# A scheduled attention and feed-forward kernel: eight DMA lanes in the plan, another load order, a PSUM bank for the rest's x, and q's exponential row by row

## The chip, the cores and the metric

The kernel runs on one core of one Trainium2 chip. The metric is the device time of one execution in microseconds (us). Five engines work side by side, each through its own instruction stream in order: TensorE (PE in the profile; its weight loads are PEld), VectorE (DVE), ScalarE (ACT), GpSimd (POOL) and SyncE (SP), which issues most of the DMA transfers.

## The reference

Four batches of eight heads, 576 tokens, 64 dimensions per head, everything in 32-bit floats:

```
q_s = softmax(q, over the 64 dims);  k_s = softmax(k, over the 576 tokens)
kv  = k_s^T v            (64 x 64 for each head);   x = q_s kv
x   = (silu(x w_gate) * (x w_val)) w_out            2304 x 512 -> 1536 -> 512
out = ((x w_a) * (x w_b)) w_out2                    2304 x 512 -> 1536 -> 512
```

The q that is put in has a spread of 0.8, k and v have one of 0.1.

## The kernel before

**Tiling.** The tokens are cut into five blocks: 512 of each batch, and the four "rests" of 64 tokens together. The first layer (l = 0) takes its blocks in the order batch 0, 1, 2, the rests, batch 3; the second (l = 1) in the order 0, 1, 2, 3, rests. In a block the hidden dimension of 1536 goes by in 12 tiles f. For each f TensorE makes two products `u_l_i_f_0` and `u_l_i_f_1` (12 matmuls of 512 columns each, since every operand is split into a high and a low part and three products are added), ScalarE and VectorE make the gated h from them (silu `s`, product into the second `u`, high part by an ACT cast, low part by a DVE subtraction), and four groups of three matmuls add h to the accumulators `acc` (the down product). The two u of a tile have one PSUM bank each, gv0 and gv1. The down product of f stands behind the two u of f + 1.

**Weights.** Each tile of weights arrives as 64-bit floats (`wr`, two halves of 768 columns, two 32-bit words each) and is converted once per layer: ACT takes an absolute value (`a<-wr`, L363) and scales the low words (`wr<-wr`, L367), DVE clamps, shifts and joins (L369, L372, L375), POOL or DVE adds (L380), then the high part is an ACT cast and the low part a subtraction on DVE or POOL (`w<-a`, L298 and L292). In the first block this conversion runs beside the products that need its result.

**Attention.** `attend(b, g, ...)` does two heads: four groups g for each batch b. Its tiles are `ut` for b < 2 and `ua`, `uc`, `uq` later. On PE: `kx` and `kb` (the maximum of k turned round), `kv`, `qt` and `ql` (q turned round), `xt` (x of 512 tokens), `xl` (x of the rest). Batch 0 runs before the first block; batch 1 is mixed into the first block, batch 2 into the second, batch 3 into the third. ACT, which computes both exp and silu, loads a function table when it changes from one to the other.

**Order.** Nothing runs in the order in which the code adds it. `Plan.add` collects operations with an estimated cost, `Plan.prepare` gives each a due time, counted back from its users and from a wanted time (`due=`), and `Plan.order` plays the engines forward in estimated time, always taking the operation that can start first, and among those the one due first. That gives each engine's order and the PSUM bank of each buffer that has several tags. On the chip each engine then runs its stream in order and waits for semaphores. Loads on SP keep the order in which the code adds them (`after=last_load`). The framework has eight DMA semaphores, and a transfer's issue waits until the one eight before has landed.

Of the kernel before, what the change touches and what calls it, by code (L numbers as in the profile page):

```python
# [30 lines left out]
class Plan:  # L31
# [11 lines left out]
    SLACK = 0.7  # L43
    DMA_START, DMA_END, DMA_RATE = 1.1, 0.95, 300e3
    TABLE = 1.3
# [69 lines left out]
    def order(self):  # L115
# [34 lines left out]
        while len(done) < len(ops):  # L150
# [27 lines left out]
            if op["table"] and op["table"] != table:  # L178
                table, t = op["table"], t + self.TABLE
            free[engine] = t + cost  # L180
            if op["nbytes"]:
                dma_free = max(dma_free, t + self.DMA_START) + op["nbytes"] / self.DMA_RATE
                end[n] = dma_free + self.DMA_END
            elif engine == "tensor":
                window = int(t / self.WINDOW)
                used[window] = used.get(window, 0.0) + cost
                full = used.get(window - 1, 0.0) > 0.3735 * self.WINDOW
                free[engine] = end[n] = t + cost * (1 if full else 2)
            else:
                end[n] = t + cost  # L190
# [21 lines left out]
def kernel(  # L212
# [201 lines left out]
    def attend(b, g, xhl, due):  # L414
# [57 lines left out]
        def qraw():  # L472
            return col(Q, q0, n)
# [90 lines left out]
        for o, x, y, keys, key, width in less:  # L564
# [11 lines left out]
        add("gpsimd", pool_us(m, BROADCAST), lambda: nc.gpsimd.tensor_tensor(
            out=qx(), in0=qraw()[:, 0:m].rearrange("p (h r d) -> p r h d", h=HG, r=R),
            in1=st()[:, 0, 0:G].rearrange("p (h r) -> p r h", h=HG).unsqueeze(3).to_broadcast([P, R, HG, D]),
            op=ALU.subtract), [QR, (st, "max")], [Q_])
        add("gpsimd", pool_us(P, BROADCAST), lambda: nc.gpsimd.tensor_tensor(  # L580
            out=ql(), in0=qr_(), in1=st()[:, 0, G:G + 1].to_broadcast([P, P]), op=ALU.subtract),
            [*QRL, (st, "maxl")], [(A, "ql")])
# [19 lines left out]
        for h in range(HG):  # L602
# [16 lines left out]
        add("vector", 0.17, lambda: nc.vector.tensor_scalar(
            out=st()[:, 2, :], in0=st()[:, 1, :], scalar1=EPS, scalar2=None, op0=ALU.add), [st], [st])  # L620
        add("vector", 0.21, lambda: nc.vector.reciprocal(out=st()[:, 3, :], in_=st()[:, 2, :]), [st], [st])  # L621
        add("gpsimd", pool_us(n, BROADCAST), lambda: nc.gpsimd.tensor_tensor(  # L622
            out=qg(), in0=qg(), in1=st()[:, 3, :].unsqueeze(2).to_broadcast([P, GX, D]), op=ALU.mult),
            [Q_, QL, st], [Q_, QL])
        pt, pl = psum([P, R, P], "qt", f"acc{g}"), psum([P, SL], "ql")
# [236 lines left out]
```

## Time and profile before

| | |
|---|---|
| median of 3 runs | 1008.91 us (1008.12 to 1010.12) |
| the profiled execution's own time | 1010.94 us |
| its span, first to last instruction | 1009.1 us |
| PE busy | 966.9 us (96%) |
| DVE, ACT, POOL busy | 411.6, 347.8, 188.1 us |
| granted TensorE clock, mean | 0.987 |

PE is busy for nearly all of the span, so its idle time is what there is to look for. It lies almost wholly ahead of 171 us, where the other three engines are busiest. Times of rows count from the span's start; between the profiled execution's time and its span lie 1.8 us.

### The profile page before, as it was taken

How to read it: one execution, taken by the hardware profiler on the slowest of the kernel's cores; microseconds unless marked ns; L12 is line 12 of the kernel's file. 1: busy time of each engine (PE TensorE's matmuls, PEld its weight loads, DVE VectorE, ACT ScalarE, POOL GpSimd, SP SyncE). 2: the span in 40 equal slices, each digit the busy share in tenths (PEclk: the TensorE clock that was granted, in tenths of full speed). 3: DMA queues.
4: the chain of work that ended last, by engine and by line, in shares of the span. 5: the costliest groups of instructions: out<-in, count | busy, mean ns of one | idle time of the engine just before them, and what ended most of it. 6: DMA issues, size and time to landing. Idle time of an engine off the chain costs nothing.

```text
span 1009.1 us, 12039 instructions
## 1 busy us (share of the span) xinstructions
PE 966.9 (96%) x4616; PEld 799.8 (79%) x4616; DVE 411.6 (41%) x702; ACT 347.8 (34%) x556; POOL 188.1 (19%) x206
## 2 busy tenths in 40 slices
PE   5679989999999999999999999999999999999997
PEld 4467667888878888898888888888888888888897
DVE  6678797433233333424666763221121112211212
ACT  5665666333332334313455551211121112111211
POOL 5654453111111110200444341000000000000000
PEclk9879999999999999999999999999999999999999
DMA  9732544210131112501334630020001001000100
GB/s 275 242 105 72 178 141 148 90 45 28 33 120 48 47 47 94 180 1 63 121 126 129 186 118 0 1 84 1 1 21 64 1 0 42 21 1 1 42 1 22
DMA packets 77137, 74.18 MB, mean 74 GB/s; under 512 B 29976, under 2 KB 64280, under 8 KB 76184
## 3 DMA queue, kind: packets, MB, share of 16 engines
q1 hardware_dynamic: 71416, 69.36, 22.3%
q10 hardware_dynamic: 5664, 4.07, 1.2%
q8 instruction: 36, 0.59, 0.2%
q14 instruction: 21, 0.17, 0.1%
HBM read 60.29 MB, written 13.11 MB: 73 GB/s over the span
## 4 chain that ended last, share of the span: by engine, by line
PE 82%; DMA 1%; ACT 1%; DVE 1%; issue 1%; POOL 0%; SPq 0%; ACTq 0%; POOLq 0%; DVEq 0%
PE u L707 53%; PE acc L737 15%; PE acc L734 12%; DMA wr<-in_moe_w_out_dram 1%; PE kv L594 1%; PE xt L642 1%; DMA out_dram<-ob 0%; PE qt L629 0%; DVE xhl L292 0%; PE kv L595 0%; PE ql L632 0%; DVE ob L750 0%; ACT wr L367 0%; ACT xhl L298 0%; SPq L341 0%
## 5 line engine op out<-in xcount | busy, mean ns | idle before, releaser
L707 PE MATMUL u<-xhl,w 128*128 128x512 f32 (+1 forms) x2856 | 625.1, 373 | 7.4 <-DVE w L292 4.4
L707 PEld LDWEIGHTS u<-xhl,w 128*128 128x128 f32 x2856 | 498.5, 190 | 105.0 <-DVE w L292 4.2
L721 DVE TENSOR_TENSOR u<-s,u 128x512 f32<-128x512 f32 (+1 forms) x120 | 77.1, 643 | 425.7 <-PE u L707 388.9
L718 ACT ACTIVATE s<-u 128x512 f32<-128x512 f32 (+1 forms) x120 | 66.8, 557 | 301.0 <-PE u L707 299.6
L734 PE MATMUL acc<-h,w 128*128 128x512 f32 (+1 forms) x720 | 167.3, 379 | 0.4 <-DVE h L292 0.2
L737 PE MATMUL acc<-w,h 128*128 128x512 f32 x648 | 157.4, 392 | 0.0
L734 PEld LDWEIGHTS acc<-h,w 128*128 128x128 f32 x720 | 125.0, 189 | 27.8 <-issue 1.9
L737 PEld LDWEIGHTS acc<-w,h 128*128 128x128 f32 x648 | 120.9, 188 | 25.6
L298 ACT CAST h<-u 128x512 fp32r<-128x512 f32 (+1 forms) x120 | 65.3, 544 | 208.3 <-DVE u L721 206.9
L380 POOL TENSOR_TENSOR a<-a,wr 128x768 uint32<-128x768 uint32 (+1 forms) x48 | 95.6, 1993 | 184.8 <-DVE a L375 165.7
L292 DVE TENSOR_TENSOR h<-u,h 128x512 fp32r<-128x512 f32 (+1 forms) x120 | 76.3, 635 | 50.1 <-ACT h L298 49.8
L292 POOL TENSOR_TENSOR xhl<-xraw,xhl 128x512 fp32r<-128x512 f32 (+1 forms) x6 | 7.3, 1220 | 340.7 <-ACT xhl L298 243.9
L375 DVE SCALAR_TENSOR_TENSOR a<-wr,a 128x768 uint32<-128x768 uint32 (+1 forms) x49 | 58.1, 1188 | 0.7
L367 ACT ACTIVATE wr<-wr 128x768 uint32<-128x768 uint32 (+1 forms) x49 | 43.8, 895 | 12.2 <-DMA wr<-in_moe_w_out_dram 12.1
L363 ACT ACTIVATE a<-wr 128x768 f32<-128x768 f32 (+1 forms) x40 | 35.5, 888 | 25.4 <-DMA wr<-in_moe_w_out_dram 22.4
L298 ACT CAST w<-a 128x768 fp32r<-128x768 f32 (+1 forms) x49 | 39.8, 816 | 8.2 <-POOL a L380 3.7
L369 DVE TENSOR_SCALAR a<-a 128x768 f32<-128x768 f32 (+1 forms) x49 | 32.8, 677 | 18.4 <-ACT a L363 18.3
L292 DVE TENSOR_TENSOR w<-a,w 128x768 fp32r<-128x768 f32 (+1 forms) x36 | 35.2, 989 | 5.0 <-ACT w L298 3.4
L292 POOL TENSOR_TENSOR w<-a,w 128x768 fp32r<-128x768 f32 (+1 forms) x13 | 23.9, 1839 | 26.2 <-ACT w L298 26.2
L372 DVE TENSOR_SCALAR a<-a 128x768 uint32<-128x768 uint32 (+1 forms) x49 | 27.7, 573 | 0.7
L622 POOL TENSOR_TENSOR ua<-ua,st 128x640 f32<-128x640 f32 x8 | 10.1, 1262 | 94.8 <-DVE st L621 94.8
L298 ACT CAST xhl<-xraw 128x512 fp32r<-128x512 f32 (+1 forms) x36 | 18.8, 572 | 15.8 <-PE u L707 9.4
(102 smaller groups left out, 426.3 us busy)
## 6 DMA issues: line engine op xcount, KB each, us to landing
wr<-in_moe_w_out_dram SPq DMA_DIRECT2D x46, 256.0 KB, 3.9
xraw<-x SPq DMA_DIRECT2D x7, 1024.0 KB
wr<-in_moe_w_a_dram SPq DMA_DIRECT2D x24, 256.0 KB, 2.9
wr<-in_moe_w_b_dram SPq DMA_DIRECT2D x24, 256.0 KB, 3.0
wr<-in_moe_w_gate_dram SPq DMA_DIRECT2D x22, 256.0 KB, 2.7
wr<-in_moe_w_val_dram SPq DMA_DIRECT2D x22, 256.0 KB, 5.7
x<-ob SPq DMA_DIRECT2D x16, 256.0 KB, 2.0
out_dram<-ob SPq DMA_DIRECT2D x16, 256.0 KB, 3.6
```

The lines of the kernel that those rows point to most:

```text
L292: engine.tensor_tensor(out=out(), in0=x(), in1=y(), op=op)
L298: add("scalar", act_us(n), lambda: nc.scalar.copy(out=hi(), in_=src()), [src_key], [hi_key])
L363: add("scalar", act_us(e) + 0.08, lambda: nc.scalar.activation(out=a().bitcast(F32), in_=high().bitcast(F32), func=AF.Abs), parts, [a], ot ...
L367: add("scalar", act_us(e) + 0.08, lambda: nc.scalar.activation(out=low(), in_=low(), func=AF.Copy, scale=2.0 ** -29), parts, [(raw, (h, "l ...
L369: add("vector", dve_us(e, 2), lambda: nc.vector.tensor_scalar(out=a().bitcast(F32), in0=a().bitcast(F32), scalar1=TOP, scalar2=LEAST, op0= ...
L375: add("vector", dve_us(e), lambda: nc.vector.scalar_tensor_tensor(out=a(), in0=high(), scalar=0xC0000000, in1=a(), op0=ALU.bitwise_and, op ...
L380: engine.tensor_tensor(out=a(), in0=a(), in1=low(), op=ALU.add)
L707: nc.tensor.matmul(ps()[:, 0:n], lhsT=wv[:, c, :], rhs=x()[:, xs, c, 0:n], start=(a == 0 and c == 0), stop=(a == 2 and c == KD - 1))
L718: add("scalar", act_us(n), lambda: nc.scalar.activation(out=s()[:, 0:n], in_=ga()[:, 0:n], func=AF.Silu if l == 0 else AF.Copy), [ga], [s] ...
L721: add("vector", dve_us(n), lambda: nc.vector.tensor_tensor(out=gb()[:, 0:n], in0=s()[:, 0:n], in1=gb()[:, 0:n], op=ALU.mult), [s, gb], [gb])
L734: nc.tensor.matmul(ps()[:, 0:n], lhsT=w()[:, 4 + ws, o * P:(o + 1) * P], rhs=h()[:, hs, 0:n], start=begin, stop=end)
L737: nc.tensor.matmul(ps(), lhsT=h()[:, hs, o * P:(o + 1) * P], rhs=w()[:, 4 + ws, :], start=begin, stop=end)
```

## The change

The planner's model of DMA gets a limit of eight transfers under way, a longer tail (1.5 for 0.95) and a slightly lower rate. The first loads come in another order: q and k of the first three groups ahead of the first tile's weights. The four attentions of batch 1 move from the tiles f = 2, 4, 6, 8 to f = 4, 5, 6, 7 in the order of the loads. The rest's x (`xl`, `py` in the code) may only take the banks at0 and at1, where batch 0 could have taken gv0 and gv1 too, and its copy gets a due time. From the second batch on q's exponential no longer shares one instruction with k's: DVE gives the maximum negated, and ACT makes nine instructions, eight of 64 columns and one of 128, each with its row's maximum as bias and its row sum as second output. The two subtractions on POOL and the row sum on DVE go away, and the normalisation on POOL is split in two.

```diff
-    DMA_START, DMA_END, DMA_RATE = 1.1, 0.95, 300e3
+    DMA_START, DMA_END, DMA_RATE, DMA_LANES = 1.1, 1.5, 290e3, 8
...
+            if op["nbytes"] and len(lanes) >= self.DMA_LANES:
+                t = max(t, lanes[-self.DMA_LANES])
...
+                lanes.append(end[n])
...
         add("vector", dve_us(m), lambda: nc.vector.tensor_reduce(
-            out=st()[:, 0, 0:G], in_=qraw()[:, 0:m].rearrange("p (g d) -> p g d", d=D), axis=AX.X, op=ALU.max),
+            out=st()[:, 0, 0:G], in_=qraw()[:, 0:m].rearrange("p (g d) -> p g d", d=D), axis=AX.X, op=ALU.max, negate=b > 0),
...
+        else:
+            K2 = [K_, KL]
+            add("scalar", act_us(n), lambda: nc.scalar.activation(
+                out=col(A, a0, n), in_=col(A, a0, n), func=AF.Exp), K2, K2, table="exp")
+            SUMS = []
+
+            def row(out, at, x, reads, key):
+                SUMS.append((st, f"sum{x}"))
+                width = P if x == G else D
+                add("scalar", act_us(width) + 0.1, lambda: nc.scalar.activation(
+                    out=out(), in_=qraw()[:, at:at + width], func=AF.Exp, bias=st()[:, 0, x:x + 1],
+                    accum_out=st()[:, 1, x:x + 1]), reads, [key, SUMS[-1]], table="exp")
+
+            for r in range(R):
+                for h in range(HG):
+                    x = h * R + r
+                    row(lambda r=r, h=h: qx()[:, r, h, :], x * D, x, [QR, (st, "max")], (A, ("q", x)))
+            row(ql, m, G, [*QRL, (st, "maxl")], QL)
...
-        add("vector", dve_us(n), lambda: nc.vector.tensor_reduce(
-            out=st()[:, 1, :], in_=qg(), axis=AX.X, op=ALU.add), [Q_, QL], [st])
+        if b == 0:
+            add("vector", dve_us(n), lambda: nc.vector.tensor_reduce(
+                out=st()[:, 1, :], in_=qg(), axis=AX.X, op=ALU.add), [Q_, QL], [st])
...
-        px, py = psum([P, SM], "xt", f"acc{g}"), psum([P, SL], "xl")
+        px, py = psum([P, SM], "xt", f"acc{g}"), Buf(pg, [P, SL], F32, ("at0", "at1"), f"xl{u}")
...
-        add("scalar", act_us(SL), lambda: nc.scalar.copy(out=oc()[:, 0:SL], in_=py()), [py], [oc])
+        add("scalar", act_us(SL), lambda: nc.scalar.copy(out=oc()[:, 0:SL], in_=py()), [py], [oc],
+            due=FIRST if due is None else due + 2)
...
-    for kind, g in (("k", 0), ("k", 1), ("q", 0), ("rest", 0), ("w", 0), ("rest", 1), ("q", 1), ("rest", 2), ("k", 2),
+    for kind, g in (("k", 0), ("rest", 0), ("k", 1), ("rest", 1), ("q", 0), ("rest", 2), ("q", 1), ("k", 2), ("q", 2),
...
-        if f % 2 == 0 and f <= 2 * KD:
-            list(attend(1, f // 2 - 1, None, FIRST + BLOCK * (f // 2 - 0.2) / KD))
+        if AHEAD <= f < AHEAD + KD:
+            g = f - AHEAD
+            list(attend(1, g, None, FIRST + BLOCK * (g + 0.8) / KD))
```

In ACT's stream before, ahead of the first silu, the rest's x of batch 0's groups 2 and 3 (`xl_399`, `xl_450`, copied to `xq`) and the last cast of the first block's x (`xhl_0`) stand behind a scaling of the fourth weight tile (`wr_3`):

```order
L636 COPY ut_106<-qt_408 128x512
L638 COPY ut_106<-ql_418 128x64
L367 ACTIVATE wr_3_332<-wr_3_332 128x768
L656 COPY xq_448<-xl_399 128x64
L298 CAST xhl_0_295<-xt_441 128x512
L657 DMA x_4_349<-xq_448 128x64
L656 COPY xq_464<-xl_450 128x64
```

The same place now:

```order
L671 COPY ut_106<-qt_383 128x512
L673 COPY ut_106<-ql_390 128x64
L302 CAST xhl_0_277<-xt_367 128x512
L371 ACTIVATE wr_3_314<-wr_3_314 128x768
L302 CAST xhl_0_277<-xt_402 128x512
L371 ACTIVATE wr_3_314<-wr_3_314 128x768
L693 DMA x_4_379<-xq_325 128x64
```

The scaling of `wr_3` stays ahead of the last cast, while the copies of the rest's x have moved behind it, and the loads of `wr_3` stand earlier on SP, ahead of batch 1's first attention instead of behind it.

A little later on ACT, around the second silu (`s_0_1`) and the first attention of batch 1 (`ut_280` before, `ut_410` now), before:

```order
L367 ACTIVATE wr_4_360<-wr_4_360 128x768
L363 ACTIVATE a_2_0_502<-wr_2_180 128x768
L367 ACTIVATE wr_5_0_427<-wr_5_0_427 128x768
L298 CAST w_0_381<-a_0_2_244 128x512
L367 ACTIVATE wr_5_1_444<-wr_5_1_444 128x768
L718 ACTIVATE s_0_1_548<-u_0_1_0_505 128x512
L586 ACT_TABLE_LOAD
L586 ACTIVATE ut_280<-ut_280 128x1280
L298 CAST w_2_571<-a_2_0_502 128x3x256
L298 CAST w_2_571<-a_2_1_510 128x3x256
```

and now:

```order
L302 CAST h_0_0_511<-u_0_0_1_412 128x512
L601 ACT_TABLE_LOAD
L601 ACTIVATE ut_410,st_493<-ut_410,st_493 128x64 x7
L601 ACTIVATE ut_410,st_493<-ut_410,st_493 128x128
L601 ACTIVATE ut_410,st_493<-ut_410,st_493 128x64
L302 CAST w_2_552<-a_2_0_465 128x3x256
L754 ACT_TABLE_LOAD
L754 ACTIVATE s_0_1_563<-u_0_1_0_478 128x512
L302 CAST w_2_552<-a_2_1_485 128x3x256
L371 ACTIVATE wr_5_0_470<-wr_5_0_470 128x768
L367 ACTIVATE a_3_0_586<-wr_3_314 128x768
L367 ACTIVATE a_3_1_594<-wr_3_314 128x768
```

The scaling of `wr_5` has moved from ahead of the second silu to behind it; q's nine rows stand ahead of that silu with a table load on each side, and k's exponential (640 columns) follows these rows with a third load.

On PE the first `kv` of batch 1 stood between the second tile's u and the first down product:

```order
L707 MATMUL u_0_1_1_550<-xhl_0_295,w_1_484 128x512 x12
L594 MATMUL kv_575<-ut_280 128x130 x4
L595 MATMUL kv_575<-ut_280 128x130
L734 MATMUL acc_0_0_584<-h_0_0_498,w_0_381 128x512 x3
L734 MATMUL acc_0_1_595<-h_0_0_498,w_0_381 128x512 x3
L734 MATMUL acc_0_2_602<-h_0_0_498,w_0_381 128x512 x3
L734 MATMUL acc_0_3_608<-h_0_0_498,w_0_381 128x512 x3
L707 MATMUL u_0_2_0_615<-xhl_0_295,w_2_571 128x512 x8
```

and now:

```order
L743 MATMUL u_0_1_1_539<-xhl_0_277,w_1_447 128x512 x12
L558 MATMUL kb_576<-ident,kr_546 128x128
L770 MATMUL acc_0_0_582<-h_0_0_511,w_0_317 128x512 x3
L770 MATMUL acc_0_1_589<-h_0_0_511,w_0_317 128x512 x3
L770 MATMUL acc_0_2_596<-h_0_0_511,w_0_317 128x512 x3
L770 MATMUL acc_0_3_603<-h_0_0_511,w_0_317 128x512 x3
L743 MATMUL u_0_2_0_608<-xhl_0_277,w_2_552 128x512 x8
L616 MATMUL kv_624<-ut_410 128x130 x4
L617 MATMUL kv_624<-ut_410 128x130
L664 MATMUL qt_632<-ident,ut_410 128x128 x4
```

`kv` has moved behind the first down product and eight matmuls of the third tile.

## Rows read from the trace of the kernel before

**Rows 1.** Stages: start:end, length, then busy time (and instructions) of each engine.

```profile
35.34:47.41 12.07, 8.10 (x26) 5.89 (x27) 5.53 (x9) 6.09 (x11) 8.19 (x9) 0.86 0.93 305
47.41:171.11 123.70, 108.94 (x472) 84.28 (x471) 103.63 (x157) 79.96 (x111) 59.48 (x54) 0.94 0.41 125
171.11:395.00 223.89, 223.85 (x1041) 181.73 (x1040) 77.50 (x174) 76.74 (x116) 29.47 (x68) 1.00 0.19 57
395.00:1009.10 614.10, 606.07 (x2988) 512.79 (x2987) 201.28 (x303) 164.53 (x281) 70.29 (x37) 1.00 0.17 54
sum 1009.10, PE 966.87 PEld 799.81 DVE 411.61 ACT 347.84 POOL 188.12; mean PE 193.37 PEld 159.96 DVE 82.32 ACT 69.57 POOL 37.62
```

**Rows 2.** PE's timeline: start, us, instruction, then idle before it and its releaser.

```profile
41.57 6.48 PE L692 MATMUL u<-xhl,w 128*128 128x512 f32 x21 [3.54 <-ACT xq L656]
49.86 1.51 PE L707 MATMUL u<-xhl,w 128*128 128x512 f32 x4 [1.81 <-DVE w L292]
...
63.13 2.10 PE L594 MATMUL kv<-ut 128*128 128x130 f32 x8 [4.67 <-ACT ut L586]
...
76.84 3.04 PE L734 MATMUL acc<-h,w 128*128 128x512 f32 x12
...
92.40 3.01 PE L707 MATMUL u<-xhl,w 128*128 128x512 f32 x12 [0.69 <-ACT s L718]
...
100.66 0.65 PE L629 MATMUL qt<-ident,ut 128*128 128x128 f32 x4 [1.33 <-POOL ut L622]
...
102.74 2.08 PE L642 MATMUL xt<-ut 128*128 128x512 f32 x2 [1.26 <-ACT ut L636]
103.83 4.40 PE L707 MATMUL u<-xhl,w 128*128 128x512 f32 x12
...
137.75 5.27 PE L707 MATMUL u<-xhl,w 128*128 128x512 f32 x22 [2.13 <-DVE w L292]
```

**Rows 3.** ACT's timeline, the same columns.

```profile
40.43 0.91 ACT L367 ACTIVATE wr<-wr 128x768 uint32<-128x768 uint32 x1 [3.63 <-DMA wr<-in_moe_w_out_dram]
41.23 0.20 ACT L656 COPY xq<-xl 128x64 f32<-128x64 f32 x1
...
57.00 0.94 ACT L367 ACTIVATE wr<-wr 128x768 uint32<-128x768 uint32 x1 [5.41 <-DMA wr<-in_moe_w_out_dram]
...
60.51 1.28 ACT L586 ACT_TABLE_LOAD   x1
61.81 1.27 ACT L586 ACTIVATE ut<-ut 128x1280 f32<-128x1280 f32 x1
...
171.11 0.60 ACT L718 ACTIVATE s<-u 128x512 f32<-128x512 f32 x1 [4.01 <-PE u L707]
```

**Rows 4.** Groups by line, ACT: count | busy, mean ns of one | idle before.

```profile
L586 ACT ACT_TABLE_LOAD x12 | 15.4, 1283 | 5.1 <-DVE ua L292 3.1 <-DMA x<-ob 1.9
L586 ACT ACTIVATE ut<-ut 128x1280 f32<-128x1280 f32 x8 | 10.2, 1274 | 2.6 <-POOL ut L580 1.7 <-DVE a L375 0.9
L610 ACT ACTIVATE ut<-kv,ks 64x64 f32<-64x64 f32 x8 | 2.5, 311 | 2.6 <-DVE ks L601 2.4 <-DVE ut L606 0.2
L638 ACT COPY uc<-ql 128x64 f32<-128x64 f32 x8 | 1.7, 212 | 2.5 <-PE ql L632 2.4
```

**Rows 5.** Groups by line, DVE and POOL, the same columns.

```profile
L375 DVE SCALAR_TENSOR_TENSOR a<-wr,a 128x768 uint32<-128x768 uint32 x46 | 56.0, 1221 | 0.7
L617 DVE TENSOR_REDUCE st<-ut 128x10 f32<-128x640 f32 x8 | 6.5, 814 | 3.6 <-ACT ut L586 3.6
...
L380 POOL TENSOR_TENSOR a<-a,wr 128x768 uint32<-128x768 uint32 x45 | 90.9, 2021 | 177.3 <-DVE a L375 159.5 <-issue 5.7 <-PE acc L734 4.6
L292 POOL TENSOR_TENSOR w<-a,w 128x768 fp32r<-128x768 f32 x11 | 21.4, 1942 | 26.2 <-ACT w L298 26.2
L622 POOL TENSOR_TENSOR ut<-ut,st 128x640 f32<-128x640 f32 x8 | 10.6, 1336 | 6.6 <-DVE st L621 3.5 <-DVE st L619 2.1 <-DVE ks L601 1.1
L576 POOL TENSOR_TENSOR ut<-ut,st 128x512 f32<-128x512 f32 x8 | 9.8, 1230 | 5.8 <-DVE st L571 5.8
```

More of the change, by code (lines that the diff above doesn't have):

```diff
@@ L123, in order @@
         dma_free, port_free, table, used, done = 0.0, 0.0, None, {}, []
+        lanes = []
         def free_at(tag):
@@ L501, in load_v @@
                     out=vx()[:, h, :, 0:D], in_=v[b, g * HG + h, 0:SM, :].rearrange("(p r) d -> p r d", r=R)),
-                    P * R * D * 4, [(C, f"v{h}")])
+                    P * R * D * 5, [(C, f"v{h}")])
         def qrl():
@@ L571, in attend @@
         add("vector", dve_us(m), lambda: nc.vector.tensor_reduce(
-            out=st()[:, 0, 0:G], in_=qraw()[:, 0:m].rearrange("p (g d) -> p g d", d=D), axis=AX.X, op=ALU.max),
+            out=st()[:, 0, 0:G], in_=qraw()[:, 0:m].rearrange("p (g d) -> p g d", d=D), axis=AX.X, op=ALU.max, negate=b > 0),
             [QR], [(st, "max")])
         add("vector", dve_us(P), lambda: nc.vector.tensor_reduce(
-            out=st()[:, 0, G:G + 1], in_=qr_(), axis=AX.X, op=ALU.max), QRL, [(st, "maxl")])
@@ L576, in attend @@
[L576 to L582, printed above, removed]
@@ L583, in attend @@
-        QL = (A, "ql")
-        KQ = [K_, KL, Q_, QL]
-        add("scalar", act_us(2 * n), lambda: nc.scalar.activation(out=kq(), in_=kq(), func=AF.Exp), KQ, KQ,
-            table="exp")
+            out=st()[:, 0, G:G + 1], in_=qr_(), axis=AX.X, op=ALU.max, negate=b > 0), QRL, [(st, "maxl")])
+        QL = (A, "ql")
+        if b == 0:
+            add("gpsimd", pool_us(m, BROADCAST), lambda: nc.gpsimd.tensor_tensor(
+                out=qx(), in0=qraw()[:, 0:m].rearrange("p (h r d) -> p r h d", h=HG, r=R),
+                in1=st()[:, 0, 0:G].rearrange("p (h r) -> p r h", h=HG).unsqueeze(3).to_broadcast([P, R, HG, D]),
+                op=ALU.subtract), [QR, (st, "max")], [Q_])
+            add("gpsimd", pool_us(P, BROADCAST), lambda: nc.gpsimd.tensor_tensor(
+                out=ql(), in0=qr_(), in1=st()[:, 0, G:G + 1].to_broadcast([P, P]), op=ALU.subtract),
+                [*QRL, (st, "maxl")], [(A, "ql")])
+            KQ = [K_, KL, Q_, QL]
+            add("scalar", act_us(2 * n), lambda: nc.scalar.activation(out=kq(), in_=kq(), func=AF.Exp), KQ, KQ,
+                table="exp")
+        else:
[14 more added lines that the diff above has]
+            row(ql, m, G, [*QRL, (st, "maxl")], QL)
@@ L614, in attend @@
         BDS = [(C, f"kvbd{h}") for h in range(HG)] + [BD]
-        add("vector", dve_us(n), lambda: nc.vector.tensor_reduce(
-            out=st()[:, 1, :], in_=qg(), axis=AX.X, op=ALU.add), [Q_, QL], [st])
-        add("vector", 0.17, lambda: nc.vector.tensor_scalar(
[L620 to L624, printed above, removed]
+        if b == 0:
+            add("vector", dve_us(n), lambda: nc.vector.tensor_reduce(
+                out=st()[:, 1, :], in_=qg(), axis=AX.X, op=ALU.add), [Q_, QL], [st])
+            sums, SUMS, QS = GX, [st], [Q_, QL]
+        else:
+            sums, QS = G + 1, [(A, ("q", x)) for x in range(G)]
+        add("vector", 0.17, lambda: nc.vector.tensor_scalar(
+            out=st()[:, 2, 0:sums], in0=st()[:, 1, 0:sums], scalar1=EPS, scalar2=None, op0=ALU.add),
+            SUMS, [(st, 2)] if b else [st])
+        add("vector", 0.21, lambda: nc.vector.reciprocal(out=st()[:, 3, 0:sums], in_=st()[:, 2, 0:sums]),
+            [(st, 2)] if b else [st], [(st, 3)] if b else [st])
+        if b == 0:
+            add("gpsimd", pool_us(n, BROADCAST), lambda: nc.gpsimd.tensor_tensor(
+                out=qg(), in0=qg(), in1=st()[:, 3, :].unsqueeze(2).to_broadcast([P, GX, D]), op=ALU.mult),
+                [*QS, st], QS)
+        else:
+            add("gpsimd", pool_us(m, BROADCAST), lambda: nc.gpsimd.tensor_tensor(
+                out=qx(), in0=qx(), in1=st()[:, 3, 0:G].rearrange("p (h r) -> p r h", h=HG).unsqueeze(3).to_broadcast(
+                    [P, R, HG, D]), op=ALU.mult), [*QS, (st, 3)], [Q_, *QS])
+            add("gpsimd", pool_us(P, BROADCAST), lambda: nc.gpsimd.tensor_tensor(
+                out=ql(), in0=ql(), in1=st()[:, 3, G:G + 1].to_broadcast([P, P]), op=ALU.mult), [QL, (st, 3)], [QL])
         pt, pl = psum([P, R, P], "qt", f"acc{g}"), psum([P, SL], "ql")
@@ L790 @@
         next(u)
-    for kind, g in (("k", 0), ("k", 1), ("q", 0), ("rest", 0), ("w", 0), ("rest", 1), ("q", 1), ("rest", 2), ("k", 2),
-                    ("q", 2), ("w", 1), ("v", 0), ("k", 3), ("q", 3), ("v", 1), ("w", 2), ("v", 2), ("v", 3)):
+    for kind, g in (("k", 0), ("rest", 0), ("k", 1), ("rest", 1), ("q", 0), ("rest", 2), ("q", 1), ("k", 2), ("q", 2),
+                    ("w", 0), ("k", 3), ("q", 3), ("v", 0), ("v", 1), ("w", 1), ("v", 2), ("v", 3), ("w", 2)):
         if kind == "rest":
```

## The prediction

> **What bounds the kernel now.** I read the stages first, then PE's waits, then what ACT did at those times. The stages [rows 1] show PE busy for 223.85 of 223.89 us between 171.11 and 395, and for 606.07 of 614.10 behind that. 171.11 is the start of the first block's last silu [rows 3]. From there PE alone sets the pace, and the change takes no product away. So the change must win or lose ahead of 171.11. PE idles 3.97 us in the stage from 35.34 to 47.41 (12.07 less 8.10) and 14.76 us in the stage from 47.41 to 171.11 (123.70 less 108.94), where DVE is busy for 103.63 and ACT for 79.96. The 14.76 are not one bottleneck but a string of waits [rows 2]: 1.81, 4.67, 0.69, 1.33, 1.26, 2.13 and smaller ones that make up 2.9. Two big ones have one cause. At 41.57 PE had waited 3.54 us for a copy `xq`: the second u needed a bank that the rest's x still held, and that copy ran only at 41.23 since ACT stood for 3.63 us in front of a scaling whose weights had not landed [rows 3]. At 63.13 `kv` had waited 4.67 us for an exponential that ACT reached at 61.81, after 5.41 us in front of weights landing at 57.00 and a table load. The planner believed those transfers to be earlier than they were; an engine in order then held up work that was ready.
>
> **First leg, to the end of the first tile's u.** It ends at 48.05 now (41.57 + 6.48, [rows 2]). The new load order gives q and k earlier, but PE, DVE and ACT are what batch 0's attention waits for, and I find the last `xt` only some 0.6 us earlier: `kb` of groups 2 and 3 now stands behind `qt` and `ql` of groups 0 and 1, which takes back what the loads give. The 3.54 us go: `xl` is out of gv1, and when ACT reaches the scaling of `wr_3`, near 37, its loads, no longer behind batch 1's attention on SP, have been in for some us. So the leg ends near 43.9, 4.1 earlier (3.5 + 0.6).
>
> **Second leg, to the end of the down product of tile 1**, now 79.88 (76.84 + 3.04, [rows 2]). I walk the new order with the durations of the rows.
> - The first product of tile 1 still waits for the second half of `w_1`, whose cast stands behind the first silu on ACT in both orders: 1.6 us (1.81 now). It starts near 45.5.
> - `kx` follows its 12 matmuls (50.3), and needs `tm`, which DVE reaches behind two joins of 1.22 us [rows 5] and seven smaller operations, at 52.8: a wait of 2.5.
> - Then `kx`, the second u and the down product of tile 0 to 59.5; tile 2 starts at 59.8, behind two POOL additions of 2.02 and two subtractions of 1.94 [rows 5]. It started at 69.65 before, but with `kv` behind it, 1.4 us.
> - `kv` has eight matmuls ahead of it and waits for k's exponential. ACT has by then two table loads around nine rows, the silu, a cast, three weight operations and a third load: it delivers at 62.6, one us late.
> - With `kv`, `qt`, `ql`, `xt`, `xl` and the rest of tile 2 the leg ends at 72.8: 6.9 us earlier than now, 2.8 won in this leg. The 4.67 us have turned into 2.5 at `kx` and 1.0 at `kv`.
>
> What I price here: nine exponentials with a bias and a row sum have no row. Below lies the plain copy of 64 columns, 212 ns; the nearest is the ACT scaling with a factor per partition, 311 ns [rows 4]; above I put a copy on top for the second output, 523 ns. I take 0.31, the row that has an operand per partition too, and 0.37 for 128 columns. The exponential of 640 columns lies between 212 ns at 64 and 1274 at 1280 columns [rows 4]: by the slope 0.72.
>
> **Third leg, to the last silu, now 171.11.** Here ACT is the risk. In the new order there are 20 table loads between the first silu and the last, 8 before: 12 x 1.283 = 15.4 us. Rows: 33 x 0.31 + 4 x 0.37 = 11.7. Four exponentials of 0.72 for 1.274: -2.2. One weight operation less, -0.9. ACT gets 24 us more: 104 for 80. DVE loses four row sums of 0.814 [rows 5] and four weight subtractions that POOL takes over, POOL loses four subtractions of 1.23, and the normalisation, now two instructions for one of 1.336, costs it some 0.4 more each. The walk on gives these waits on PE: 1.1 at tile 4 (its second u behind a late h), 2.5 and 1.3 at tile 7 (two loads, rows of two groups, then the late h and the cast of `w_7`), the rest 3.8 in pieces under one us. That is 8.7 where the trace has 7.6 after 79.88 (0.69 + 1.33 + 1.26 + 2.13 [rows 2] and 2.2 of the smaller ones). So 1.1 is given back: the last silu comes 5.8 earlier. At 103.83, after waits of 1.33 and 1.26, 12 matmuls take 4.40 that take 3.01 at 92.40 [rows 2]; the stage's granted clock is 0.94 [rows 1]. I leave the clock out, because the new order has waits too.
>
> **The other edits.** Behind 171.11 the same nine rows and two more loads per attention go in. The cover is ACT's idle time, 76.74 busy of 223.89 [rows 1]. Between one silu and the next lie 24 matmuls and 12 of the down product, some 8.2 us (rows of 12 take 3.0 [rows 2] and overlap by about 0.25); in a tile with rows ACT needs 0.6 + 1.3 + 0.37 + 8 x 0.31 + 1.3 and 0.6 for the h cast, 6.7, so 1.5 remain. `kv` behind k's exponential has some 1.2 us left by the same count. I cost this at nothing; the cover is thin. The lane limit, DMA tail and due times act only through the order.
>
> **Sum.** -4.1 - 2.8 + 1.1 = -5.8, say 6, against the profiled 1010.94, which is the span of 1009.1 and 1.8 around it: 1004.9. That execution lies 2.0 above the median of the runs, so the median is forecast at **1003**.
>
> **A rule that speaks against it.** The trace has table loads of 1283 ns, and the instruction behind one starts 1.30 us after it (60.51 to 61.81, [rows 3, 4]). The Trainium skill, page "ScalarE: Activation LUTs", section "What ACT_TABLE_LOAD costs", adds a drain of about 1380 ns to each load, 2.66 us for a switch, and says under "Table sets: the hidden batching unit" to batch calls by set. By that price the 12 added loads of the third leg would cost some 32 us and not 15. The rows here show no such drain.
>
> **Rivals.**
> - *ACT takes the first block.* Of its 43.7 idle us in the stage (123.70 - 79.96, [rows 1]) a third may not be avoidable (waits for weights). With rows of 0.523 (37 x 0.21 = 8 more) ACT takes 104 + 8 + 15 = 127 from 43.3 on: the last silu at 170, 1 us earlier, 1008. For it: 24 us more on an engine in order. Against it: PE and DVE take most of a 120 us stretch too, and ACT's work for weights can run ahead.
> - *Switching tables costs more than the load.* If ACT stood as long again at each load, as that rule has it, the third leg has 20 x 1.3 = 26 more: 104 + 26 = 130, and with some 10 of waits the last silu falls at 183, 12 late: slower, 1015 with a part hidden by idle time. It decides from about 0.7 us per load on, where 14 us more eat the idle time that my walk leaves and the 6 won. Against it stands the 1.30.
> - *The waits nearly all go.* If relief of DVE and POOL and the earlier weights count for more than my walk says, 3.97 + 14.76 less some 4 of them go: 15 less, 994. For it: DVE is the busiest of the three in this stage. Against: it needs ACT not to be late anywhere.
> - *The change does nothing:* not possible for the 3.54, since `xl` can't take gv1 any more; but the next wait could be as long: this is in the first rival's price.
>
> **How the numbers follow.** A measurement of this kernel can tell about 0.2%, 2.0 us, from no change: 1006.9 to 1010.9. Chances: my forecast 0.60 (its own range 998.5 to 1007.5, that is 4.5 each way for the third leg, of which a twentieth falls in "no change"), ACT takes the block 0.15, switching or longer rows make it slower 0.10, nearly all waits go 0.15. Faster 0.57 + 0.15 = 0.72; same 0.15 + 0.03 = 0.18; slower 0.10. The range from 996 to 1010 leaves out the slower case and about half of the best.
>
> **What the profile would show.** First leg: no wait of PE for an `xq` copy; the first tile's u ends near 44; ACT waits for no weights between 37 and 60. Second: PE waits at `kx` for `tm`, `kv` waits one us or so; down product of tile 1 ends near 73. Third: mean of the 64-column exponentials near 0.31; ACT busy over 100 between the first and the last silu; last silu near 165; PE full behind it. I am wrong if ACT's loads have idle time behind them, if rows take 0.5, if PE waits for s or h behind 171, or if weights land later than ACT asks for them, since SP's order is a chain and one late buffer holds all loads behind it.

## The result and the profile after

The changed kernel takes **1002.25 us** (median of 4 runs, 1000.51 to 1002.42) beside 1009.51 for the kernel before in the same session (4 runs, 1008.12 to 1010.14): a ratio of 0.9917 (95% interval 0.9898 to 0.9936), faster by 0.6 to 1.0%. The profiled execution took 1002.42 us with a span of 1000.5, which is 8.6 shorter than before. The forecast was 1003.0, range 996 to 1010.

Stages of the kernel after, start:end, length, then busy time and instructions of PE, PEld, DVE, ACT, POOL, then the granted clock. They answer to [rows 1]. The second row ends where PE ends the first product of the first block's last tile; that is what the silu at 171.11 had waited for in the kernel before, so the two stages end at the same point of the work.

```profile
33.19:40.63 7.44, 7.09 (x31) 4.93 (x29) 7.44 (x11) 6.11 (x10) 4.41 (x8) 1.00 0.78 251
40.63:163.86 123.23, 107.83 (x470) 83.80 (x471) 99.22 (x154) 102.17 (x194) 61.12 (x58) 0.94 0.46 141
163.86:388.00 224.14, 224.07 (x1043) 182.13 (x1042) 72.59 (x169) 117.16 (x276) 17.20 (x58) 1.00 0.18 53
```

From the first block's start to that product, PE was busy for 117.04 us and idle for 18.73 before (the first two rows of [rows 1]). Now it is busy for 114.92 and idle for 15.75. With a start 2.15 earlier (33.19 for 35.34) that is 2.15 + 2.98 + 2.12 = 7.25 us up to this point. The 2.12 of busy time are the same products at a higher rate, above all those of the first tile: its 21 matmuls take 5.04 us (below) where [rows 2] has 6.48, at a granted clock of 1.00 in the first stage where [rows 1] has 0.86. The other 1.35 of the 8.6 were won behind it; that is less than executions of one kernel differ by (1008.12 to 1010.14 for the kernel before), and no run shows where it comes from. PE is still full from there on (224.07 of 224.14), with ACT now busy for 117.16 us.

PE's timeline after (start, us, instruction, idle before it and its releaser), for [rows 2]:

```profile
35.54 5.04 PE L728 MATMUL u<-xhl,w 128*128 128x512 f32 x21
42.18 0.70 PE L743 MATMUL u<-xhl,w 128*128 128x512 f32 x2 [1.60 <-ACT w L302]
43.76 2.56 PE L743 MATMUL u<-xhl,w 128*128 128x512 f32 x10 [0.88 <-DVE w L296]
51.20 0.69 PE L553 MATMUL kx<-ident,tm 128*128 128x128 f32 x2 [4.88 <-DVE tm L296]
...
56.46 3.04 PE L770 MATMUL acc<-h,w 128*128 128x512 f32 x12
59.33 2.01 PE L743 MATMUL u<-xhl,w 128*128 128x512 f32 x8
61.18 1.05 PE L616 MATMUL kv<-ut 128*128 128x130 f32 x8
...
67.65 3.05 PE L770 MATMUL acc<-h,w 128*128 128x512 f32 x12
```

The first tile's u ends at 40.58 (35.54 + 5.04) with no wait for an `xq` copy. The new wait is that of `kx` for `tm`, 4.88 us; `kv` at 61.18 waits for nothing, where it had waited 4.67. The first down product, that of tile 0, ends at 59.50 (56.46 + 3.04), that of tile 1 at 70.70. Before, the first one ended at 69.81:

```profile
65.31 4.50 PE L734 MATMUL acc<-h,w 128*128 128x512 f32 x12
```

So 10.3 us are won by the first down product, and 7.25 are left at the end of the block.

ACT's timeline after, around the first rows and at the last silu, for [rows 3]:

```profile
47.10 1.28 ACT L601 ACT_TABLE_LOAD   x1
48.40 0.35 ACT L601 ACTIVATE ut<-ut,st 128x64 f32<-128x64 f32 x1
48.65 0.19 ACT L601 ACTIVATION_READ_ACCUMULATOR ut<-ut,st 128x1 f32 x1
48.74 0.34 ACT L601 ACTIVATE ut<-ut,st 128x64 f32<-128x64 f32 x1
...
59.86 0.74 ACT L594 ACTIVATE ut<-ut 128x640 f32<-128x640 f32 x1
...
163.46 1.28 ACT L601 ACT_TABLE_LOAD   x1 [3.34 <-DMA uq<-in_q_dram]
164.75 0.35 ACT L601 ACTIVATE ua<-uq,st 128x64 f32<-128x64 f32 x1
165.01 0.19 ACT L601 ACTIVATION_READ_ACCUMULATOR ua<-uq,st 128x1 f32 x1
165.21 1.28 ACT L754 ACT_TABLE_LOAD   x1
166.51 0.60 ACT L754 ACTIVATE s<-u 128x512 f32<-128x512 f32 x1
```

Groups of ACT after, from the first silu to the last (count, then busy us, mean ns), for [rows 4]:

```profile
L754 ACT ACT_TABLE_LOAD x10 | 12.8, 1283 | 0.2
L601 ACT ACTIVATE ut<-ut,st 128x64 f32<-128x64 f32 x32 | 10.8, 338 | 0.1
L601 ACT ACT_TABLE_LOAD x8 | 10.3, 1283 | 3.5 <-DMA uq<-in_q_dram 3.3
L594 ACT ACTIVATE ut<-ut 128x640 f32<-128x640 f32 x4 | 2.9, 733 | 0.0
L594 ACT ACT_TABLE_LOAD x2 | 2.6, 1283 | 0.0
L601 ACT ACTIVATE ut<-ut,st 128x128 f32<-128x128 f32 x4 | 1.6, 399 | 1.2 <-DVE st L578 1.1
```

20 table loads, as counted from the order; a row takes 338 ns, 399 with 128 columns, and the next starts 0.33 to 0.34 later.

### The profile page after: what moved, and what is told of

The parts are those of the page before. It is cut to its first block, busy times and chain, and to the rows that moved or that the text cites. A ratio compares the mean times of both kernels' runs of the same rounds, so it can differ in the third digit from the quotient of the medians.

```text
span 1000.5 us, 12235 instructions
## 1 busy us (share of the span) xinstructions
PE 961.3 (96%) x4616; PEld 796.3 (80%) x4616; DVE 402.0 (40%) x693; ACT 409.2 (41%) x796; POOL 172.2 (17%) x193
## 4 chain that ended last, share of the span: by engine, by line
PE 83%; DMA 4%; ACT 4%; SPq 3%; DVE 2%; POOL 2%; issue 1%; POOLq 0%; DVEq 0%; ACTq 0%
PE u L743 53%; PE acc L773 15%; PE acc L770 12%; POOL a L384 2%; DMA ut<-in_k_dram 1%; DMA wr<-in_moe_w_gate_dram 1%; DMA wr<-in_moe_w_out_dram 1%; SPq L345 1%; PE kv L616 1%; PE xt L677 1%; DVE a L379 1%; SPq L504 1%; ACT L754 1%; ACT L601 1%; ACT a L367 0%
## 5 line engine op out<-in xcount | busy, mean ns | idle before, releaser
L743 PE MATMUL u<-xhl,w 128*128 128x512 f32 (+1 forms) x2856 | 624.4, 373 | 11.2 <-DVE w L296 7.2
L770 PE MATMUL acc<-h,w 128*128 128x512 f32 (+1 forms) x720 | 165.2, 376 | 1.1 <-ACT ob L786 0.8
L379 DVE SCALAR_TENSOR_TENSOR a<-wr,a 128x768 uint32<-128x768 uint32 (+1 forms) x49 | 52.0, 1062 | 0.5
L371 ACT ACTIVATE wr<-wr 128x768 uint32<-128x768 uint32 (+1 forms) x49 | 43.9, 897 | 3.0 <-DMA wr<-in_moe_w_out_dram 3.0
L296 DVE TENSOR_TENSOR w<-a,w 128x768 fp32r<-128x768 f32 (+1 forms) x37 | 39.1, 1061 | 5.6 <-ACT w L302 4.0
L376 DVE TENSOR_SCALAR a<-a 128x768 uint32<-128x768 uint32 (+1 forms) x49 | 30.3, 623 | 0.8
L601 ACT ACTIVATE ua<-uq,st 128x64 f32<-128x64 f32 (+1 forms) x72 | 24.6, 344 | 0.1
```

Source lines behind the costliest of these rows:

```text
L296: engine.tensor_tensor(out=out(), in0=x(), in1=y(), op=op)
L371: add("scalar", act_us(e) + 0.08, lambda: nc.scalar.activation(out=low(), in_=low(), func=AF.Copy, scale=2.0 ** -29), parts, [(raw, (h, "l ...
L379: add("vector", dve_us(e), lambda: nc.vector.scalar_tensor_tensor(out=a(), in0=high(), scalar=0xC0000000, in1=a(), op0=ALU.bitwise_and, op ...
L601: add("scalar", act_us(width) + 0.1, lambda: nc.scalar.activation(out=out(), in_=qraw()[:, at:at + width], func=AF.Exp, bias=st()[:, 0, x: ...
L743: nc.tensor.matmul(ps()[:, 0:n], lhsT=wv[:, c, :], rhs=x()[:, xs, c, 0:n], start=(a == 0 and c == 0), stop=(a == 2 and c == KD - 1))
L770: nc.tensor.matmul(ps()[:, 0:n], lhsT=w()[:, 4 + ws, o * P:(o + 1) * P], rhs=h()[:, hs, 0:n], start=begin, stop=end)
```

## The experiments

The change has four parts that can be taken apart: the **order** (batch 0's loads and the place of batch 1's attentions), the **figures** (lanes, tail, rate, and the bytes that the plan counts for a load of v, raised from 4 to 5 per element), the **rows** and the **bank** (with the copy's due time). Since a planner sets the order on the engines, taking one part out moves all of it. First each part was undone alone, then each was made alone. Theory "order" said that the order wins and the rows are neutral; "relief" that the rows win by easing VectorE; "loads" that the added table loads cost part of it.

**Rows undone** (the same for subtraction, sums and normalisation):

```diff
-            add("scalar", act_us(n), lambda: nc.scalar.activation(
-                out=col(A, a0, n), in_=col(A, a0, n), func=AF.Exp), K2, K2, table="exp")
+            add("scalar", act_us(2 * n), lambda: nc.scalar.activation(out=kq(), in_=kq(), func=AF.Exp), KQ, KQ,
+                table="exp")
```

> The changed kernel with q's exponential, subtraction and sums of the second batch on as before (one exponential of 1280 columns on ScalarE, subtraction on GpSimd, row sums on VectorE); load order, place of the attentions, figures and bank stay changed. Theory 'order' (the 8.6 us come from which work is put where, and the rows are worth nothing by themselves because the time that they take off VectorE and GpSimd is spent again on ScalarE's table loads): 1001 to 1004, within 0.2% of the changed kernel at 1002. Rival 'relief' (VectorE, 99 busy of 123 us in the stage ahead of the last silu, sets the pace there, and four row sums of 0.81 us and the subtractions off its neighbours make the gain): 1005 to 1009. Rival 'loads' (the 12 more table loads of 1.28 us cost the first block some of what the order wins): 996 to 1000.

**Order undone:**

```diff
-        if AHEAD <= f < AHEAD + KD:
-            g = f - AHEAD
-            list(attend(1, g, None, FIRST + BLOCK * (g + 0.8) / KD))
+        if f % 2 == 0 and f <= 2 * KD:
+            list(attend(1, f // 2 - 1, None, FIRST + BLOCK * (f // 2 - 0.2) / KD))
```

and the old list of loads.

> The changed kernel with the old order of batch 0's loads and the old place of batch 1's attentions among the tiles. Theory 'order': most of the gain goes, 1006 to 1010; the first tile's u ends 1 to 3 us later than 40.6, and ScalarE stands in front of weights that have not landed ahead of 60 us. Rival 'relief': 1001 to 1004, since the rows stay.

**Figures undone:**

```diff
-    DMA_START, DMA_END, DMA_RATE, DMA_LANES = 1.1, 1.5, 290e3, 8
+    DMA_START, DMA_END, DMA_RATE, DMA_LANES = 1.1, 0.95, 300e3, 10 ** 6
```

and v's bytes counted by 4 again.

> The changed kernel with the planner's transfers priced as before (no limit of lanes, tail 0.95, rate 300e3, v's bytes by 4). Theory 'order': ScalarE is again put in front of weights ahead of 60 us for some 2 to 5 us, of which a part reaches the end: 1003 to 1007. Rival 'relief' and rival 'loads': no difference, 1001 to 1003.

**Bank undone:**

```diff
-        px, py = psum([P, SM], "xt", f"acc{g}"), Buf(pg, [P, SL], F32, ("at0", "at1"), f"xl{u}")
+        px, py = psum([P, SM], "xt", f"acc{g}"), psum([P, SL], "xl")
```

and the copy without its due time.

> The changed kernel with the rest's x of each attention again in any free bank of four and its copy without a due time. Theory 'order': the second u of the first tile waits for a copy xq again, but not as long, since ScalarE no longer stands in front of weights there: 0.5 to 3.5 us back, 1003 to 1006. Rival 'relief': the same wait of 3.5 us as before at most, and else no difference: 1002.

**Each part alone**, the same edits the other way round on the kernel before:

> The kernel before with only batch 0's loads in the new order and batch 1's attentions at the new place among the tiles; rows, figures and bank stay old. Theory 'any one' (the old order held two stalls in a row, 3.54 us for xq and 4.67 us at kv behind weights that had not landed, with a clock of 0.83 behind them; each edit alone moves ScalarE's work so far that the longer one goes): 1002 to 1005. Rival 'together' (two edits must come together, since each alone leaves one of the two stalls): 1006 to 1009.

> The kernel before with only the planner's transfers priced as in the change (8 lanes, tail 1.5, rate 290e3, v's bytes by 5). Theory 'any one': ScalarE no longer stands in front of weights for 5.41 us, 1002 to 1006. Rival 'together': 1006 to 1009.

> The kernel before with only q's exponential row by row from the second batch on. Theory 'any one': k's exponential no longer waits for q's subtraction and is half as long, kv waits less than 4.67 us: 1003 to 1006. Rival 'together': the stall at kv comes from weights in front of the table load, which stays: 1007 to 1010. Rival 'loads': the added table loads make it 1010 to 1014.

> The kernel before with only the rest's x of each attention in the attentions' own two banks and its copy due later. The prediction's first leg gives 3.5 us for this, 1005 to 1006. Theory 'any one': the wait for xq goes, and what stands behind it waits as before for converted weights, so that a part comes back: 1004 to 1008. Rival 'together': all of it comes back behind the first tile: 1008 to 1010.

**Two and two:**

> The kernel before with two of the four edits: loads and attentions in the new order, and the new figures for transfers; rows and bank stay old. Theory 'late weights': what counts is whether ScalarE is put in front of weights that land later. With both, SP sends tile 5's weights ahead of batch 1's attentions and the plan has them late enough: no such wait, 1001 to 1005. Rival 'three needed': the wait is still there, 1008 to 1012.

> The kernel before with the other two edits: rows and bank; loads, attentions and figures stay old. Theory 'late weights': the plan still thinks tile 5's weights landed and puts their scaling ahead of work that is ready: a wait of 5 us or so at 50 to 58 us, 1008 to 1013. Rival 'three needed': the same. Rival 'bank and rows' (the two stalls that the prediction priced, at xq and at kv, are the ones that these two edits take away): 1002 to 1005.

What was measured, with the change itself in the last row. The ratio is to the kernel before in the same session (medians 1009.50 for the kernels with one part undone, 1009.85 for those with one alone, 1010.27 for the pairs), and is not the quotient of the two medians (for order with figures that would be 0.9927). "Joins" is the number of 128x768 weight joins (half a tile each) that DVE had started by 80 us of the profiled execution; before, it was 6. "First down product" is where PE ended it in that execution; before, at 69.81.

| parts made | median us | ratio (95% interval) | joins | first down product, us |
|---|---|---|---|---|
| order | 1013.02 | 1.0031 (1.0018 to 1.0045) | 7 | 77.04 |
| figures | 1009.64 | 0.9988 (0.9976 to 0.9999) | 7 | 68.36 |
| rows | 1012.46 | 1.0028 (1.0017 to 1.0039) | 6 | 72.67 |
| bank | 1010.12 | 0.9995 (0.9983 to 1.0007) | 6 | 70.02 |
| rows, bank | 1009.27 | 0.9995 (0.9983 to 1.0007) | 7 | 70.66 |
| order, figures | 1002.89 | 0.9945 (0.9923 to 0.9967) | 8 | 60.65 |
| order, figures, bank | 1003.25 | 0.9930 (0.9915 to 0.9946) | 8 | 64.15 |
| figures, rows, bank | 1003.93 | 0.9939 (0.9921 to 0.9956) | 8 | 58.27 |
| order, rows, bank | 1002.37 | 0.9926 (0.9910 to 0.9941) | 8 | 63.60 |
| order, figures, rows | 1000.94 | 0.9910 (0.9893 to 0.9928) | 8 | 61.87 |
| all four | 1002.25 | 0.9917 (0.9898 to 0.9936) | 8 | 59.50 |

Three things follow. The best part by itself, the figures, wins 0.12%; order and rows alone lose 0.3%. The parts don't add up: their four changes alone sum to +0.4%, together they give -0.8%. And none of the four is needed: with any one undone the kernel is within the interval of the change, or close to it. So "order", as theory for one part, fell, as "any one" and "three needed" did; "relief" fell as the source of the gain (rows undone keeps it, rows alone lose 0.3%). With the rows undone 9 table loads stand between 35 and 170 us where the change has 22, and the kernel is not faster; but undoing the rows takes back DVE's relief along with ACT's loads, so that shows only that the two together are worth little. That each counts and they cancel is not excluded. "Together" comes nearest: order and figures together are enough; but not any two, since rows and bank together win nothing.

**What the gainers share.** The last two columns separate them without exception. By 80 us 8 joins had started in all six that gain and 6 or 7 in the six that don't, the kernel before among them. PE's first down product ends at 58.27 to 64.15 in the six that gain and at 68.36 or later in the others, so the lead is there well ahead of 80 us. Groups of DVE up to 80 us, first of the kernel after, then of order with figures, then of rows with bank:

```profile
L379 DVE SCALAR_TENSOR_TENSOR a<-wr,a 128x768 uint32<-128x768 uint32 x8 | 9.5, 1198 | 0.0
```

```profile
L379 DVE SCALAR_TENSOR_TENSOR a<-wr,a 128x768 uint32<-128x768 uint32 x8 | 11.0, 1378 | 0.1
```

```profile
L379 DVE SCALAR_TENSOR_TENSOR a<-wr,a 128x768 uint32<-128x768 uint32 x7 | 6.4, 939 | 0.0
```

A tile of the first block takes 123.23 / 11 = 11.2 us, so half a tile of converted weights is some 5.6 us of PE's work (an estimate from the stage above). One or two halves more by 80 us is the size of the gain. This is a mark of a lead, seen in each profile, and no cause by itself. The kernel with the rows doubled, below, has 8 joins by 80 us too and its first down product ends at 64.25, and it loses later: by 100 us it has started 10 joins, as have all that gain nothing, where the six that gain have started 12. Why each mixture gets its lead is not shown.

**The first leg's stall is not it.** With the bank undone, and with order and figures alone, PE waits for `xq` as long as before and the first tile's u ends at 47, not 41. PE's timeline of these two kernels, in this order:

```profile
40.56 6.60 PE L727 MATMUL u<-xhl,w 128*128 128x512 f32 x21 [4.15 <-ACT xq L691]
50.31 4.60 PE L742 MATMUL u<-xhl,w 128*128 128x512 f32 x12 [3.15 <-ACT s L753]
```

```profile
40.56 6.46 PE L696 MATMUL u<-xhl,w 128*128 128x512 f32 x21 [4.27 <-ACT xq L660]
...
50.50 0.45 PE L558 MATMUL kb<-ident,kr 128*128 128x128 f32 x1 [3.15 <-DVE kr L556]
```

Both are as fast as the change within overlapping intervals (1000.94 and 1002.89), so the end of this stall is not needed for the gain. From 40 to 80 us, the stretch with this stall, DVE was busy for 31.86 and 37.38 us in them and for 26.78 in the kernel before: I read it as conversion that went on while PE stood, and spared PE waits later. That is not shown: with rows and bank, which gain nothing, DVE was busy there for 31.80 us.

**One wait taken away directly.** After the first eight runs another mark stood out: in all that gained nothing ACT waited 5.3 to 6.7 us for a `w_out` between 45 and 58 us, in those that gained at most 1.2. So in the kernel before that one scaling was held back behind k's exponential of batch 1's first attention, which `behind` names:

```diff
         add("scalar", act_us(e) + 0.08, lambda: nc.scalar.activation(
-            out=low(), in_=low(), func=AF.Copy, scale=2.0 ** -29), parts, [(raw, (h, "low"))])
+            out=low(), in_=low(), func=AF.Copy, scale=2.0 ** -29), parts, [(raw, (h, "low"))],
+            after=behind if (l, f) == (0, 5) else ())
```

> The kernel before with one thing held back: on ScalarE the scaling of tile 5's first weights (wr_5_0) is put behind k's exponential of batch 1's first attention, by one order dependency; with it tile 5's second scaling falls behind. In all five kernels that gained nothing ScalarE stands 5.3 to 6.7 us in front of a w_out that has not landed, between 45 and 58 us, and in none of the five that gained does it stand there over 1.2 us. Theory 'late weights' (this one wait on ScalarE, with the 4.67 us at kv and the clock of 0.83 that follow it, is most of what the change removes): 1002 to 1006, PE's wait at kv under 1.5 us. Rival 'moves on' (held back, the weights are late for the tiles behind or PE waits for converted weights instead, and the change's gain needs its whole new order): 1008 to 1011.

It took 1008.62 us, a ratio of 0.9993 (0.9977 to 1.0008): no difference. Its ACT timeline:

```profile
58.15 0.60 ACT L721 ACTIVATE s<-u 128x512 f32<-128x512 f32 x1 [0.77 <-PE u L710]
60.77 1.28 ACT L587 ACT_TABLE_LOAD   x1 [2.03 <-DVE ut L292]
62.07 1.27 ACT L587 ACTIVATE ut<-ut 128x1280 f32<-128x1280 f32 x1
```

The 5.41 us in front of weights [rows 3] are gone and the exponential still starts at 62.07 (61.81 before): what ACT now waits for is DVE's subtraction for the same attention. But this execution was late ahead of the place of the edit. Its first tile began 0.9 later (36.28 for 35.34) and the first tile's u ended 2.3 later (50.36 for 48.05), and DVE's subtraction came 2.3 later too, first before, then held back:

```profile
57.51 0.88 DVE L292 TENSOR_TENSOR ut<-ut,kb 128x512 f32<-128x512 f32 x2
```

```profile
59.82 0.88 DVE L292 TENSOR_TENSOR ut<-ut,kb 128x512 f32<-128x512 f32 x2
```

PE's wait at `kv` is 2.48 us for 4.67. From the end of the first tile's u to the end of the first down product it took 18.76 us for 21.76, so 3.0 us were won there in this execution and 2.3 of them had been lost ahead of it; 7 joins had started by 80 us. By the median and its interval the wait by itself is worth at most 0.23%, some 2.3 us of the 7 to 9. "Late weights" fell as an account of most of the gain, and "moves on" held: behind the wait that the trace named stood another. With the figures alone the same wait is still 5.32 us, so pricing the transfers anew did not by itself remove it. The two pairs agree with the mark as far as it goes (the wait is 1.69 us with order and figures and 3.71 with rows and bank), so that it counts beside other things is not excluded.

**Rows doubled**, in the changed kernel's own order; each row is issued twice and the second writes the same values:

```diff
-                add("scalar", act_us(width) + 0.1, lambda: nc.scalar.activation(
+                add("scalar", act_us(width) + 0.1, lambda: [nc.scalar.activation(
                     out=out(), in_=qraw()[:, at:at + width], func=AF.Exp, bias=st()[:, 0, x:x + 1],
-                    accum_out=st()[:, 1, x:x + 1]), reads, [key, SUMS[-1]], table="exp")
+                    accum_out=st()[:, 1, x:x + 1]) for _ in range(2)], reads, [key, SUMS[-1]], table="exp")
```

> The changed kernel, in its own order, with each of its 108 row exponentials issued twice in a row (the second writes the same values again). Adds 108 x 0.33 to 0.40 us to ScalarE, 12 us ahead of the last silu and 24 behind it. The prediction's cover behind the first block is 1.5 us in a tile with rows, and 8 rows more take 2.7: by it PE waits some 1.2 us in each of 8 tiles, and ahead of the last silu a third to a half of 12 us shows: 1010 to 1018. Rival 'cover is thick' (the cover is the whole idle time of ScalarE, 107 of 224 us, since it can run ahead of PE): only the part ahead of the last silu shows, 1004 to 1009.

It took 1020.79 us, ratio 1.0117 (1.0098 to 1.0137): slower than either theory said. PE's timeline of the last tile in the first block, first after, then with the rows doubled:

```profile
161.17 5.30 PE L743 MATMUL u<-xhl,w 128*128 128x512 f32 x22 [1.42 <-DVE w L296]
```

```profile
173.84 5.30 PE L743 MATMUL u<-xhl,w 128*128 128x512 f32 x22 [1.41 <-DVE w L296]
...
183.13 3.33 PE L770 MATMUL acc<-h,w 128*128 128x512 f32 x12 [1.09 <-ACT h L302]
...
192.78 2.11 PE L743 MATMUL u<-xhl,w 128*128 128x512 f32 x8 [0.71 <-ACT s L754]
...
297.77 3.32 PE L770 MATMUL acc<-h,w 128*128 128x512 f32 x12 [1.19 <-ACT h L302]
```

The 32 + 4 rows ahead of it add 32 x 0.338 + 4 x 0.399 = 12.4 us to ACT, and the tile starts 12.67 later. That the two numbers are alike is in part chance. From the first block's start to this tile, first after, then with the rows doubled (columns as in the stages):

```profile
33.19:161.17 127.98, 112.24 (x490) 86.52 (x488) 105.92 (x162) 107.88 (x203) 65.53 (x65) 0.95 0.48 148
```

```profile
33.74:173.84 140.10, 117.45 (x489) 89.45 (x488) 106.51 (x161) 122.76 (x275) 65.49 (x65) 0.90 0.44 135
```

Of the 12.67 us, 0.55 lie ahead of the block and so ahead of the rows; PE is idle for 6.91 more (22.65 for 15.74), and busy for 5.21 more with the same products, at a granted clock of 0.90 for 0.95. So in the new order work put on ACT ahead of the last silu does come out at the end, a good half of it as PE's waiting and the rest as slower matmuls. Behind it PE has waits at `h` and `s` again, the three shown 2.99 us: the cover there is thin, as the prediction had it (by its count PE would wait 1.2 us in each of eight tiles), and a thicker one ("the whole idle time of ACT") is excluded. From the last tile to the first product of the rests this kernel needs 5.94 us more (414.80 - 173.84 for 396.19 - 161.17): 3.62 of it is idle time, and 2.32 is busy time that no row explains.

Why then does undoing the rows win nothing? From 40 to 170 us, first after, then with the rows undone (columns as in the stages):

```profile
40.00:170.00 130.00, 114.48 (x498) 88.47 (x496) 101.66 (x157) 108.86 (x205) 61.75 (x58) 0.95 0.45 137
```

```profile
40.00:170.00 130.00, 114.08 (x486) 87.54 (x485) 110.83 (x167) 78.22 (x109) 62.06 (x60) 0.93 0.45 137
```

ACT goes from 108.86 to 78.22, DVE from 101.66 to 110.83, and PE does the same. The rows move the load from DVE to ACT, 9 us off the one for 31 on the other. That ACT sets the pace with the rows is what the doubled ones speak for; that DVE is so without them is argued from its 110.83 of 130 us alone. No version tried beats the change beyond its interval; bank undone has the lowest median, 1000.94, with overlapping intervals.

## Why the prediction was right, and where it wasn't

The total was right, 1003.0 for 1002.25, in part by luck. The legs were off by 3.4 us to one side and by 1.1 and 0.8 to the other, and 1.35 behind the block were not forecast: the two profiled executions lie 8.6 us apart where the sum had 5.8. And the sum prices PE's waits one by one, which the experiments contradict.

| step | forecast | measured |
|---|---|---|
| first leg, end of the first u | 43.9 (4.1 won) | 40.58 (7.5 won) |
| second leg, end of the down product of tile 1 | 72.8 (6.9 won in all) | 70.70 (9.2) |
| third leg, to the last silu's product | 5.8 won in all | 7.25 |
| behind it | nothing | 1.35 won |

- **First leg.** The 3.54 us at `xq` went as forecast, and ACT waited for no weights between 37 and 60. The last `xt` came 2.3 us earlier (34.43 for 36.74), not 0.6: I had let `kb` behind `qt` take back too much. The 21 matmuls' higher rate I had not counted. But the step itself, "the 3.54 us go, so 3.5 are won", is what the experiments contradict: the bank alone is worth 0.05%, and two kernels that keep the stall are as fast. A wait of PE was priced as if nothing else would hold PE afterwards. The rest of my sum is as fragile.
- **Second leg.** The wait at `kx` was 4.88, not 2.5, though `kx` came earlier than forecast (51.20 for 52.8): PE had its 12 matmuls behind it at 46.32 (forecast 50.3), and `tm`, begun at 49.10, took 2.04 us instead of 0.42 (below). `kv` waited for nothing where I had 1.0: k's exponential started at 59.86 and has 640 columns. Tile 2 started at 59.33, forecast 59.8.
- **Third leg.** 20 table loads, the rows' price (338, 399, 733 ns for 310, 370, 720) and ACT's load (102.17 us in the stage, forecast 104 to the last silu) held. 1.9 us were given back here (9.2 to 7.25) for 1.1. The wait at tile 7 was 2.81 for 2.5, the one at tile 4 nearly absent. The last silu came at 166.51, behind a table load ahead of which ACT had stood 3.34 us for q to land, a row and a second table load; PE had other work meanwhile and stayed full, so it cost nothing.
- **Behind it.** PE stays full with the rows and loads on ACT, as costed at nothing; that the cover is thin is shown by the doubled rows.
- **The rivals.** "Switching costs more than the load" is out: the row behind the load of 47.10 starts at 48.40, 1.30 later, as before. "ACT takes the first block" was half right: work added to ACT does lengthen the block (12.1 us for 12.4 added, waits and slower matmuls together), though the 22 us more than before (102.17 for 79.96) did not eat the gain. The first leg's u at a granted clock of 1.00 for 0.86 won 1.4 us that the prediction, which left the clock out, didn't have. "The waits nearly all go" did not happen: 15.75 us of idle time are left in the block.

The cause, as far as it is settled: the gain lies in the first block (7.25 of 8.6 us); no single part makes it, order with figures does, rows with bank doesn't. It comes with a first down product that ends 4 us or more ahead of those of all kernels that gain nothing, and with one to two more half tiles of weights joined by 80 us. Open is what brings each mixture there. The four pairs of one of order or figures with one of rows or bank were not run, nor the two halves of the order apart.

## What to carry to other kernels

Where several engines feed PE and a planner sets all orders, a wait in PE's timeline is not a price: ask what the feeding engines do during it, since what they get done there comes back later. Measure the parts of such a change both alone and left out, because their worth may lie only in the mixture. To find out whether a side engine sets the pace, double a small piece of its work in the fixed order; a busy share (102 of 123 us here) would not have told that 12.4 us more make the block 12.1 longer. Then split what it cost into idle and busy time of the main engine, for here only 6.9 of it were waits.

## What the hardware showed that was not expected

The same maximum `tm` of 128x256 took 0.41 to 2.04 us on DVE. After, at 49.10, first DVE, then POOL:

```profile
47.37 1.81 DVE L379 SCALAR_TENSOR_TENSOR a<-wr,a 128x768 uint32<-128x768 uint32 x2
49.10 2.04 DVE L296 TENSOR_TENSOR tm<-ut 128x256 f32<-128x256 f32 x1
51.07 0.68 DVE L296 TENSOR_TENSOR h<-u,h 128x512 fp32r<-128x512 f32 x1
```

```profile
48.45 4.40 POOL L384 TENSOR_TENSOR a<-a,wr 128x768 uint32<-128x768 uint32 x2 [0.73 <-DVE a L379]
```

POOL's two additions begin at 48.45 and take 4.40, so `tm`, with two operands, ran beside them and is 1.6 us longer than its shortest. `kx` and so PE waited for it. The Trainium skill, page "SBUF — State Buffer", section "SBUF: two separate sides", says that a DVE operation with two SBUF inputs and a GpSimd operation that reads SBUF exclude each other for a whole instruction; this row agrees with that.

A row with a sum brings a second instruction of 188 ns, ACTIVATION_READ_ACCUMULATOR. It overlaps the row (48.65 in a row that runs from 48.40 to 48.75), and the next row starts at 48.74, while it is still running, so it does not hold up the next row. What a row takes without a sum, no run shows.
